# Attention and two expert layers on one core: a third query and key buffer, nine product buffers, weight conversion from slot 2

## The chip, the cores and the metric

The kernel runs on one core of a Trainium2 chip. The metric is device time in microseconds from start to end of one execution; the median of three timed runs of the kernel before is 641.99 us.

## The reference

Three layers run one after the other on 2304 tokens (4 batches of 576) of 512 values. The first is attention with 8 heads of 64: four heads look at the last 32 positions, four at every 32nd. The second multiplies by three matrices, takes the largest of the three products and multiplies by `w_out`. The third sends each token to the best of eight experts.

```python
def _attn_ref(q, k, v):
    ...
    scores = np.where(masks[None, :, :, :], scores, -1000000000.0)
    scores = scores - np.max(scores, axis=-1, keepdims=True)
    attn = np.exp(scores)
    attn = attn / (np.sum(attn, axis=-1, keepdims=True) + 1e-09)
    return np.matmul(attn, v)

def _moe_ref(x, w1, w2, w3, w_out):
    h = np.maximum(np.maximum(x @ w1, x @ w2), x @ w3)
    return h @ w_out

def _moe2_ref(x, modality_id, w_gate, modality_bias, w1, w2):
    logits = x @ w_gate + modality_bias[modality_id]
    e_idx = np.argmax(logits, axis=1)
    ...
        h = np.maximum(x[mask] @ w1[e], 0.0)
        out[mask] = gate_w[mask, None] * (h @ w2[e])
```

## The kernel before

Products are made from a high and a low half of each operand, three matmuls for one (`mm3`). Tokens are taken in six blocks of 384. For block j, `L1(j, f)` makes slice f (of six) of the first product of the second layer: three groups of twelve matmuls, m = 0, 1, 2, with the largest kept in `t1s`. `L2(j)` multiplies the six slices by `w_out` and gets six groups of eighteen. The slices of a block lie in `chunks`, buffers of 768 columns, taken in turn (`h_of`): eleven before.

Everything else is put between these matmul groups. `slot()` is one step of it; a list written out by hand in the last lines of the program decides how many slots there are, and the engines' queues take instructions in the order in which `slot()` writes them. Attention is cut into 40 groups. In a slot with a tick, slot t, group t gets its scores (`att_S`, TensorE), group t-1 its max and bias (VectorE), t-2 its exponential (ScalarE), t-3 its reciprocal (VectorE) and multiplication (GpSimd), t-4 its transposes, and t-5 its product with the values; the result of t-5 is written as a high half (`att_hi`, ScalarE) and a low half (`att_lo`, VectorE), and L1 reads both.

The weights of the second layer come as 24 pieces of 512 KB with 64-bit words and are converted to 32 bit. A slot with conversion takes piece i: the absolute value on ScalarE (`conv_abs`, line 366), four VectorE operations on piece i-1 (`conv_ops`, lines 378, 381, 383, 385; the last one frees the staging buffer, of which there are three, and the next piece is loaded), and the split of piece i-2 (line 397 on ScalarE, 398 on GpSimd). Pieces 18 to 23 are `w_out`; each also gets a transpose (`gate_T`, line 405) and four small matmuls (`gate_G`, line 411), which fold the experts' gate into `w_out`. These gate slots take accumulator banks from the same round as L1: two banks while conversion goes on, three afterwards (`mm_bank`).

The first thirteen slots are the prologue. No L1 runs there, since its first block needs groups 0 to 7; `keep_warm` puts four matmuls without use behind each slot. Before, conversion starts at slot 4 (`CS`). Loads are issued by the SyncE queue in the order of the slots: in slot t the next piece, the values of group t-2, and the queries and keys of group t+2 if that group is the first of a head pair. The two buffers `qk_b` hold a head pair each.

Of the kernel before, what the change touches and what calls it, by code (L numbers as in the profile page):

```python
# [10 lines left out]
F32 = mybir.dt.float32  # L11
F32R = mybir.dt.float32r
# [13 lines left out]
NF = DFF // 128  # L26
# [80 lines left out]
def tile_attention_moe_moe(ctx: ExitStack, tc: tile.TileContext, qk, vw, w, wg, ids, bias, e12, cst, out):  # L107
    nc = tc.nc
    PE, ACT, DVE, POOL, SP = nc.tensor, nc.scalar, nc.vector, nc.gpsimd, nc.sync
    sb = ctx.enter_context(tc.tile_pool(name="sb", bufs=1))  # L110
# [2 lines left out]
    W = sb.tile([128, 18432], F32R, name="W")  # L113
    R = sb.tile([128, 16384], F32R, name="R")
    HT = sb.tile([128, 4608], F32R, name="HT")
    HX = sb.tile([128, 3072], F32R, name="HX")
    stage = sb.tile([128, 3, 2, 512], F32, name="stage")
    y = sb.tile([128, NS, ROW], F32, name="y")
    t1s = sb.tile([128, 2, TB], F32, name="t1s")
# [32 lines left out]
    xh = R[:, xo:xo + KD * XR].rearrange("p (k t) -> p k t", k=KD)  # L152
    xl = R[:, xo + KD * XR:xo + 2 * KD * XR].rearrange("p (k t) -> p k t", k=KD)
    spare = R[:, xo + 2 * KD * XR:xo + 2 * KD * XR + 768]
    chunks = [z[:, 768 * i:768 * i + 768] for z, n in ((HT, 6), (HX, 4)) for i in range(n)] + [spare]

    def h_of(j, f):
        return chunks[(NF * j + f) % 11].rearrange("p (s t) -> p s t", s=2)

    ht = [HT[:, 768 * i:768 * i + 768].rearrange("p (s t) -> p s t", s=2) for i in range(6)]  # L160
    ht2 = ht + [W[:, 16384 + 768 * i:16384 + 768 * i + 768].rearrange("p (s t) -> p s t", s=2) for i in range(2)]
    at_pool = tc.tile_pool(name="at", bufs=1)
    AT = at_pool.__enter__().tile([128, 5504], F32, name="AT")
    qk_b = [AT[:, 1216 * i:1216 * i + 1216].rearrange("p (s n) -> p s n", s=2) for i in range(2)]
    v_b = [AT[:, 2432 + 384 * i:2432 + 384 * i + 384].rearrange("p (c d) -> p c d", c=3) for i in range(3)]
    s_b = [AT[:, 3584 + 384 * i:3584 + 384 * i + 384] for i in range(3)]
    pt_b = [AT[:, 4736 + 384 * i:4736 + 384 * i + 384].rearrange("p (c q) -> p c q", c=3) for i in range(2)]

    ew = [
        [z[:, o:o + 8192].rearrange("p (f m n) -> p f m n", f=NF2, m=2) for o in (0, 8192)]  # L170
# [15 lines left out]
    NG = len(groups)  # L186
    st = {}

    def load_qk(i):
        if i < NG and groups[i][2] == 0:  # L190
            b, p, _ = groups[i]
            SP.dma_start(qk_b[p % 2], qk[b, p])

    def load_v(i):
        if i < NG:
# [4 lines left out]
    def units(p, g):  # L200
        if p < 2:
            return [3 * g, 3 * g + 1, 3 * g + 2], 96
        return ([0, 3, 1, 4, 2, 5] if g == 0 else [6, 9, 7, 10, 8]), 54
# [3 lines left out]
    def mask_of(p, g, n):  # L207
        if p < 2:
            o = 0 if g == 0 else 96
            return mask[:, o:o + 288].rearrange("p (u k) -> p u k", k=96)  # L210
        return mask[:, None, 384:438].to_broadcast([128, n, 54])

    def s_view(i):
        b, p, g = groups[i]
        us, w_ = units(p, g)
        n = len(us)
        ps = bank[3 + i % 2][:, :n * w_].rearrange("p (u k) -> p u k", k=w_)
        wide = s_b[i % 3].rearrange("p (u k) -> p u k", k=96 if p < 2 else 64)
        m = mx[:, i % 4, :, :n]
        top = m[:, 0] if i in ON_DVE else bank[3 + i % 2][:, 400:400 + n]  # L220
        return ps, wide[:, :n, :w_], (top, m[:, 1], m[:, 2], m[:, 3]), n, w_
# [3 lines left out]
    def att_S(i):  # L225
        b, p, g = groups[i]
        us, _ = units(p, g)
        t = qk_b[p % 2]
        ps, _, _, n, w_ = s_view(i)
        pe = b < MASK_ON_PE  # L230
        if pe:
            PE.matmul(ps, lhsT=identb, rhs=mask_of(p, g, n))
        for c, u in enumerate(us):
            q0 = (64 if p < 2 else 54) * u
            for r in halves:
                PE.matmul(ps[r, c], lhsT=t[r, 0, q0:q0 + 64], rhs=t[r, 1, q0:q0 + w_], start=not pe, stop=True,  # L236
                          skip_group_check=pe)
# [108 lines left out]
    NW = NF * 3 + NF  # L346
# [4 lines left out]
    def load_piece():  # L351
        i = step["load"]
        if i < NW:
            step["load"] += 1
            SP.dma_start(stage[:, i % 3].rearrange("p a n -> p (a n)").bitcast(I32),
                         w[i].bitcast(I32))
# [8 lines left out]
    def conv_abs(i):  # L365
        ACT.activation(out=wbuf(i), in_=f32(conv_words(i)[1]), func=AF.Abs)
# [35 lines left out]
    def gate_T(a):  # L402
        ps = mm_bank()
        for kk in range(KD):
            PE.transpose(ps[:, 128 * kk:128 * kk + 128], a[:, 128 * kk:128 * kk + 128], ident)
        next_slot.append(lambda: ACT.copy(gate_t, ps))
# [11 lines left out]

    now = [0]
    DEPTH = 5  # L420
    CS, FILL = 4, 16
    later, delayed, next_slot = [], [], []

    def flush():
        while later:
            later.pop(0)()

    def slot(ticks=True, conv=True):

        flush()  # L430
        while next_slot:
            next_slot.pop(0)()
        t = now[0]
        i = step["conv"]
        ticks = ticks and t < NG + DEPTH
        conv = conv and i < NW + 3
        if ticks:
            now[0] += 1
        if conv:
            step["conv"] += 1  # L440
        at = lambda fn, d: fn(t - d) if ticks and 0 <= t - d < NG else None
        ops = conv_ops(i - 1) if conv else iter(())
        at(att_exp, 2)
        at(att_eps, 3)
        if conv and i < NW:
            conv_abs(i)
        next(ops, None)
        at(att_rec, 3)
        at(att_mul, 3)
        next(ops, None)  # L450
        at(att_max, 1)
        next(ops, None)
        at(att_bias, 1)
        for _ in ops:
            pass
        if conv and 0 <= i - 2 < NW:
            conv_split(i - 2)
        more = [delayed.pop() for _ in delayed[:]]

        def rest():  # L460
            if conv and NF * 3 <= i - 3 < NW:
                gate_G(i - 3 - NF * 3, bank[3 + t % 2][:, 384:384 + E])
            if conv and NF * 3 <= i - 2 < NW:
                gate_T(wbuf(i - 2))
            at(att_T, 4)
            at(att_V, 5)
            at(att_S, 0)
            at(att_pt, 4)
            at(att_hi, 5)
            at(att_lo, 5)  # L470
            for fn in more:
                fn()
            if ticks:
                if t >= 2:
                    load_v(t - 2)
                if t:
                    load_qk(t + 2)

        later.append(rest)

    mmi = [0]
# [363 lines left out]
    with tc.manual_schedule():  # L845
# [13 lines left out]
                PE.matmul(bank[0], lhsT=warm[:, :128], rhs=warm[:, :512])  # L859

        DVE.memset(t1s, 0.0)
        POOL.memset(AT[:, 3584:4736], 0.0)
        keep_warm(9)
        POOL.memset(filler, 1.0)
        for t in range(LEAD + DEPTH):
            slot(conv=t >= CS)
            flush()
            keep_warm(4)
            if t == 1:
                for v_ in range(2):  # L870
                    DVE.tensor_scalar(out=isf[:, v_], in0=idt[:, :, 0], scalar1=float(v_), scalar2=None, op0=ALU.is_equal)
                wide = lambda v_: isf[:, v_, :, None].to_broadcast([128, NT // 128, E])
                rep = lambda v_: bb[:, v_, None, :].to_broadcast([128, NT // 128, E])
                other = rt.rearrange("p a s e -> p (a s) e")
                POOL.tensor_tensor(out=ball, in0=wide(0), in1=rep(0), op=ALU.mult)
                POOL.tensor_tensor(out=other, in0=wide(1), in1=rep(1), op=ALU.mult)
                POOL.tensor_tensor(out=ball, in0=ball, in1=other, op=ALU.add)
            if t == 2:
                for _ in range(3):
                    load_piece()  # L880

# [4 lines left out]
        for j in range(NB):  # L888
            parts = [(L1, j, f) for f in range(NF)]
            if j:  # L890
                parts.insert(NF - 1 if j == 1 else 1, (L2, j - 1))
            n = sum(3 if p_[0] is L1 else 2 * NS for p_ in parts) - 2
            start = now[0]
            k = 0
            for fn, *arg in parts:
                for _ in fn(*arg):
                    k += 1
                    if FILL <= fills < FILL + E:
                        e_ = fills - FILL
                        SP.dma_start(xs[NT * e_:NT * e_ + TB].rearrange("(p s) (h n) -> p (s h) n", p=128, h=2),  # L900
                                     filler[:, None, :].to_broadcast([128, 2 * NS, ROW // 2]))
                    fills += 1
                    due = goal.get(j, start)
                    pieces = 10 + 12 * k // 16 if j == 0 else NW + 3
                    slot(now[0] < min(due, start - (start - due) * k // n), fn is L1 and step["conv"] < pieces)
                    background(6 if j == NB - 1 else 4)
                    if j == NB - 1 and arg[-1] >= 2 and fn is L1 and not behind and wts is None:
                        open_phase2()
                        load_rows(sp_val(e0i[0:1, 3:4], E * NT - TB))
                        wts = Weights(sp_val(e0i[0:1, 1:2], E - 1), 0)  # L910
# [58 lines left out]
```

## Time and profile before

| | us |
|---|---|
| median of three runs | 641.99 (641.83 to 642.63) |
| profiled execution | 642.13 |
| its span | 640.4 |
| TensorE busy (matmul) | 614.0 |
| VectorE busy | 257.6 |
| ScalarE busy | 229.9 |
| GpSimd busy | 136.0 |

The span runs from the first instruction to the last; the profiled execution's own time is 1.7 us longer. In the profile PE is TensorE (PEld its weight loads), DVE VectorE, ACT ScalarE, POOL GpSimd, and SPq the queue of SyncE, which issues loads. A start is in microseconds from the span's start; what stands in brackets is the engine's idle time before the instruction and what ended it.

### The profile page before, as it was taken

What the parts mean: (1) busy time and instruction counts of PE and PEld (TensorE: products, weight loads), DVE (VectorE), ACT (ScalarE), POOL (GpSimd) and SP (SyncE); (2) the same over time, 40 slices, a digit from 0 to 9 for tenths busy, and PEclk for the clock granted to TensorE, in tenths of its full rate; (3) what the DMA queues carried; (4) which work ended last, traced back from release to release, by engine and by line L of the source; (5) the groups of instructions that cost most, each with busy time, mean ns of one, the idle gap of its engine ahead of it and who ended that gap; (6) DMA issues with size and microseconds to landing.
All of it is one profiled execution on the core that took longest, in us unless ns stands there. A gap on an engine that the chain in (4) does not pass through costs nothing. (4 is left out here: it accounts for less than half of the span.)

```text
span 640.4 us, 11891 instructions
## 1 busy us (share of the span) xinstructions
PE 614.0 (96%) x4597; PEld 564.7 (88%) x4603; DVE 257.6 (40%) x701; ACT 229.9 (36%) x694; POOL 136.0 (21%) x157
## 2 busy tenths in 40 slices
PE   8889998999999999999999999999999999999992
PEld 4568988899999999999999999998998979898981
DVE  4987995331334333442131133374344215331210
ACT  2868755332244334333121111342343124422220
POOL 2445553221121321142112112101101010111000
PEclk9989999999999999999999999999999999999996
DMA  7686459982021312010000004244432127220201
GB/s 245 223 280 228 131 188 241 192 137 65 1 82 58 108 52 76 21 69 10 10 18 34 1 12 171 59 138 153 151 111 89 44 77 242 83 67 33 68 19 39
DMA packets 30668, 64.44 MB, mean 101 GB/s; under 512 B 3328, under 2 KB 14336, under 8 KB 30592
## 3 DMA queue, kind: packets, MB, share of 16 engines
q1 hardware_dynamic: 27712, 54.01, 29.6%
q0 software_dynamic: 2880, 9.46, 3.9%
q8 instruction: 43, 0.70, 0.5%
q14 instruction: 33, 0.27, 0.1%
HBM read 47.68 MB, written 15.77 MB: 99 GB/s over the span
## 5 line engine op out<-in xcount | busy, mean ns | idle before, releaser
L494 PE MATMUL bank<-R,W 128*128 128x384 f32 (+1 forms) x1350 | 253.3, 343 | 3.3 <-DVE t1s L513 2.0
L494 PEld LDWEIGHTS bank<-R,W 128*128 128x128 f32 x1350 | 235.8, 188 | 9.5 <-DVE t1s L513 3.0
L494 PE MATMUL bank<-R,HT 128*128 128x260 f32 (+1 forms) x540 | 89.9, 316 | 0.3 <-POOL HT L505 0.3
L513 DVE TENSOR_TENSOR t1s<-bank,t1s 128x384 f32<-128x384 f32 x72 | 40.1, 557 | 122.0 <-PE bank L494 120.8
L494 PEld LDWEIGHTS bank<-R,HT 128*128 128x128 f32 x540 | 78.0, 188 | 6.8 <-POOL HT L505 0.5
L717 POOL DMA_INDIRECT out_dram<-y,gi x18 | 18.0, 999 | 158.7 <-ACT x2h L698 94.9
L494 PE MATMUL bank<-x2h,R 128*128 128x384 f32 x192 | 49.5, 336 | 1.1 <-ACTq L925 1.1
L277 POOL TENSOR_TENSOR AT<-AT,mx 128x288 f32<-128x288 f32 (+2 forms) x40 | 27.1, 677 | 110.2 <-DVE mx L273 103.4
L494 PE MATMUL bank<-x2h,W 128*128 128x384 f32 x192 | 49.8, 337 | 0.0
L709 DVE SCALAR_TENSOR_TENSOR HT<-bank,HT 128x384 fp32r<-128x384 f32 x36 | 20.0, 557 | 64.0 <-ACT HT L708 63.7
L262 ACT ACTIVATE AT<-bank,mx 128x96 f32<-128x96 f32 (+1 forms) x138 | 42.9, 331 | 2.9 <-DVE R L415 1.7
L716 ACT ACTIVATE y<-bank,gi 128x512 f32<-128x512 f32 x18 | 12.4, 688 | 78.1 <-PE bank L494 64.7
L494 PE MATMUL bank<-W,HT 128*128 128x512 f32 x162 | 38.5, 391 | 0.0
L505 POOL TENSOR_TENSOR HT<-t1s,HT 128x384 fp32r<-128x384 f32 x21 | 21.3, 1014 | 72.9 <-ACT HT L504 72.8
L494 PEld LDWEIGHTS bank<-x2h,R 128*128 128x128 f32 x192 | 34.7, 188 | 1.6 <-ACTq L925 1.5
L494 PEld LDWEIGHTS bank<-W,HT 128*128 128x128 f32 x162 | 30.1, 188 | 6.0
L236 PE MATMUL bank<-AT 64*64 64x54 f32 (+1 forms) x640 | 31.2, 236 | 4.1 <-DMA AT<-in_qk_dram 3.4
L494 PEld LDWEIGHTS bank<-x2h,W 128*128 128x128 f32 x192 | 34.8, 188 | 0.3 <-issue 0.3
L708 ACT ACTIVATE HT<-bank 128x384 fp32r<-128x384 f32 x36 | 17.7, 492 | 47.0 <-PE bank L494 39.0
L236 PEld LDWEIGHTS bank<-AT 64*64 64x64 f32 x640 | 24.6, 134 | 10.4 <-DMA AT<-in_qk_dram 4.3
L343 DVE TENSOR_TENSOR R<-bank,R 128x162 fp32r<-128x162 f32 (+2 forms) x56 | 20.6, 397 | 32.2 <-ACT R L339 31.8
L511 ACT COPY t1s<-bank 128x384 f32<-128x384 f32 x36 | 17.3, 480 | 43.3 <-PE bank L494 38.6
(157 smaller groups left out, 807.1 us busy)
## 6 DMA issues: line engine op xcount, KB each, us to landing
stage<-in_w_dram SPq DMA_DIRECT2D x24, 512.0 KB, 4.1
stage<-in_e_dram SPq DMA_DIRECT2D x48, 256.0 KB, 3.7
AT<-in_qk_dram SPq DMA_DIRECT2D x15, 608.0 KB, 5.2
xs<-filler SPq DMA_DIRECT2D x8, 771.0 KB, 17.3
rows<-xs SPq DMA_DIRECT2D x7, 771.0 KB, 4.6
AT<-in_vw_dram SPq DMA_DIRECT2D x24, 144.0 KB, 3.4
AT<-in_vw_dram SPq DMA_DIRECT2D x16, 192.0 KB, 3.8
AT<-in_qk_dram SPq DMA_DIRECT2D x1, 352.0 KB, 4.6
```

Source lines behind the costliest of these rows:

```text
L236: PE.matmul(ps[r, c], lhsT=t[r, 0, q0:q0 + 64], rhs=t[r, 1, q0:q0 + w_], start=not pe, stop=True, skip_group_check=pe)
L262: ACT.activation(out=s3[:, c], in_=ps[:, c], func=AF.Exp, scale=0.125, bias=m[1][:, c:c + 1], accum_out=m[2][:, c:c + 1])
L277: POOL.tensor_tensor(out=s3, in0=s3, in1=m[3][:, :, None].to_broadcast([128, n, w_]), op=ALU.mult)
L343: DVE.tensor_tensor(out=l, in0=src, in1=f32(h), op=ALU.subtract)
L494: PE.matmul(ps, lhsT=a, rhs=b_, start=i == 0, stop=i == n - 1)
L505: POOL.tensor_tensor(out=h[:, 1], in0=t1, in1=f32(h[:, 0]), op=ALU.subtract)
L511: ACT.copy(t1, ps)
L513: DVE.tensor_tensor(out=t1, in0=ps, in1=t1, op=ALU.max)
L708: ACT.activation(out=h[:, 0], in_=ps, func=AF.Relu)
L709: DVE.scalar_tensor_tensor(out=h[:, 1], in0=ps, scalar=0.0, in1=f32(h[:, 0]), op0=ALU.max, op1=ALU.subtract)
L716: ACT.activation(out=y[:, s, :DM], in_=ps, func=AF.Copy, scale=gi[:, s, 0:1])
L717: POOL.indirect_dma_start(out=out[:, :], out_offset=bass.IndirectOffsetOnAxis(ap=gi[:, s, 1:2].bitcast(I32), axis=0), in_=y[:, s, :DM], in ...
```

## The change

There are three query and key buffers instead of two, taken in turn over all head pairs (`qk_of`), and a head pair is loaded three slots ahead instead of two. The space comes from the slices: nine buffers instead of eleven. With nine, L2 of block 0 stands behind the third slice of block 1, where it stood behind the fifth. Conversion starts at slot 2 (`CS`), the first three pieces are loaded one by one in slots 0 to 2 instead of together in slot 2, and the cap on converted pieces during block 0 is written anew: 11 pieces by the end of the prologue where there were 9, 21 by the end of block 0 where there were 23.

```diff
-    HX = sb.tile([128, 3072], F32R, name="HX")
+    HX = sb.tile([128, 1536], F32R, name="HX")
...
-    chunks = [z[:, 768 * i:768 * i + 768] for z, n in ((HT, 6), (HX, 4)) for i in range(n)] + [spare]
+    chunks = [z[:, 768 * i:768 * i + 768] for z, n in ((HT, 6), (HX, 2)) for i in range(n)] + [spare]
...
-        return chunks[(NF * j + f) % 11].rearrange("p (s t) -> p s t", s=2)
+        return chunks[(NF * j + f) % 9].rearrange("p (s t) -> p s t", s=2)
...
-    qk_b = [AT[:, 1216 * i:1216 * i + 1216].rearrange("p (s n) -> p s n", s=2) for i in range(2)]
+    qk_b = [AT[:, 1216 * i:1216 * i + 1216].rearrange("p (s n) -> p s n", s=2) for i in range(3)]
...
+    def qk_of(b, p):
+        return qk_b[(4 * b + (p + 2) % 4) % 3]
+
     def load_qk(i):
         if i < NG and groups[i][2] == 0:
             b, p, _ = groups[i]
-            SP.dma_start(qk_b[p % 2], qk[b, p])
+            SP.dma_start(qk_of(b, p), qk[b, p])
...
-    CS, FILL = 4, 16
+    CS, FILL = 2, 16
...
                 if t:
-                    load_qk(t + 2)
+                    load_qk(t + 3)
...
-            if t == 2:
-                for _ in range(3):
-                    load_piece()
+            if t < 3:
+                load_piece()
...
-                parts.insert(NF - 1 if j == 1 else 1, (L2, j - 1))
+                parts.insert(3 if j == 1 else 1, (L2, j - 1))
...
-                    pieces = 10 + 12 * k // 16 if j == 0 else NW + 3
+                    pieces = 11 + 10 * k // 17 if j == 0 else NW + 3
```

What this does to the queues shows at three places. The first is SyncE's queue at the start of the program; `in_qk` is queries and keys, `in_vw` values, `in_w` weight pieces, and the rows begin with the load for group 2. Before:

```order
L192 DMA AT<-in_qk_dram 128x1216
L851 DMA wgt<-in_wg_dram 128x32
L852 DMA bb<-in_bias_dram 128x16
L853 DMA y<-in_ids_dram 128x36
L198 DMA AT<-in_vw_dram 128x384
L192 DMA AT<-in_qk_dram 128x1216
L355 DMA stage<-in_w_dram 128x1024 x3
L198 DMA AT<-in_vw_dram 128x384 x2
L192 DMA AT<-in_qk_dram 128x1216
L355 DMA stage<-in_w_dram 128x1024
```

The same place after the change:

```order
L195 DMA AT<-in_qk_dram 128x1216
L854 DMA wgt<-in_wg_dram 128x32
L855 DMA bb<-in_bias_dram 128x16
L856 DMA y<-in_ids_dram 128x36
L358 DMA stage<-in_w_dram 128x1024
L195 DMA AT<-in_qk_dram 128x1216
L358 DMA stage<-in_w_dram 128x1024
L201 DMA AT<-in_vw_dram 128x384
L358 DMA stage<-in_w_dram 128x1024 x2
L201 DMA AT<-in_vw_dram 128x384
L195 DMA AT<-in_qk_dram 128x1216
```

The first weight piece now stands where the first load of values stood, and each further piece has a load of queries and keys or of values ahead of it.

The second place is VectorE's queue in slots 3 and 4 of the prologue: `mx` holds max, sum and reciprocal of a group, `y` the words of a piece, `bank_82` the piece half converted. Before:

```order
L268 TENSOR_REDUCE mx<-AT 128x6
L269 TENSOR_SCALAR mx<-mx 128x6
L273 RECIPROCAL mx<-mx 128x6
L244 TENSOR_REDUCE mx<-bank_83 128x6
L252 TENSOR_TENSOR bank_83<-bank_83,mx 128x324
L268 TENSOR_REDUCE mx<-AT 128x5
L269 TENSOR_SCALAR mx<-mx 128x5
L273 RECIPROCAL mx<-mx 128x5
```

After the change, from the same row on:

```order
L271 TENSOR_REDUCE mx<-AT 128x6
L272 TENSOR_SCALAR mx<-mx 128x6
L381 TENSOR_SCALAR y<-y 128x512
L276 RECIPROCAL mx<-mx 128x6
L384 TENSOR_SCALAR bank_82<-y 128x512
L247 TENSOR_REDUCE mx<-bank_83 128x6
L386 SCALAR_TENSOR_TENSOR bank_82<-stage,bank_82 128x512
L255 TENSOR_TENSOR bank_83<-bank_83,mx 128x324
L388 SCALAR_TENSOR_TENSOR y<-stage,bank_82 128x512
L271 TENSOR_REDUCE mx<-AT 128x5
```

The four conversion operations stand between the steps of the attention groups, the first of them ahead of the reciprocal and the max.

The third place is TensorE's queue where the last gate slots end, early in block 1; `bank_80` to `bank_82` are the accumulators of L1 and of the transposes. Before:

```order
L405 MATMUL bank_80<-cs,y 128x128 x4
L494 MATMUL bank_81<-R,W 128x384 x12
L411 MATMUL bank_83<-wgt,gate_t 128x8 x4
L405 MATMUL bank_80<-cs,w_96 128x128 x4
L494 MATMUL bank_81<-R,W 128x384 x6
L494 MATMUL bank_82<-R,W 128x384 x6
L411 MATMUL bank_83<-wgt,gate_t 128x8 x4
L494 MATMUL bank_82<-R,W 128x384 x6
```

After the change:

```order
L408 MATMUL bank_80<-cs,y 128x128 x4
L497 MATMUL bank_81<-R,W 128x384 x12
L414 MATMUL bank_83<-wgt,gate_t 128x8 x4
L408 MATMUL bank_80<-cs,w_96 128x128 x4
L497 MATMUL bank_81<-R,W 128x384 x12
L414 MATMUL bank_83<-wgt,gate_t 128x8 x4
```

A row of twelve is the second half of one L1 group and the first half of the next in the same bank. Behind the last transpose (the one from `w_96`) the group before changed to bank 82; after the change it stays in bank 81.

## Rows read from the trace of the kernel before

**Rows 1.** Windows: length; busy us of PE, PEld, DVE, ACT, POOL; clock; DMA; GB/s.

```profile
0.00:45.00 45.00, 37.27 (x460) 22.83 (x466) 34.10 (x98) 26.81 (x92) 18.33 (x26) 0.96 0.71 246
45.00:87.00 42.00, 41.87 (x408) 38.08 (x406) 36.90 (x86) 30.33 (x106) 21.53 (x21) 1.00 0.61 197
87.00:124.00 37.00, 32.75 (x256) 29.57 (x257) 21.70 (x48) 16.40 (x46) 13.54 (x13) 1.00 0.93 204
124.00:620.00 496.00, 493.72 (x3442) 467.66 (x3441) 164.88 (x472) 155.02 (x449) 80.61 (x96) 1.00 0.25 74
```

**Rows 2.** The timeline of PE at the prologue's end (start, us, operation, idle before).

```profile
36.13 1.16 PE L236 MATMUL bank<-AT 64*64 64x54 f32 x24 [2.32 <-DMA AT<-in_qk_dram]
37.22 1.89 PE L859 MATMUL bank<-t1s 128*128 128x512 bf16 x4
...
44.14 1.04 PE L859 MATMUL bank<-t1s 128*128 128x512 bf16 x4
44.82 3.52 PE L494 MATMUL bank<-R,W 128*128 128x384 f32 x18
```

**Rows 3.** The timeline of SP, the issuing of loads.

```profile
4.79 0.43 SPq L198 DMA_DIRECT2D AT<-in_vw_dram  x1
...
9.57 1.38 SPq L355 DMA_DIRECT2D stage<-in_w_dram  x3
...
26.58 0.38 SPq L198 DMA_DIRECT2D AT<-in_vw_dram  x1
...
30.48 0.42 SPq L192 DMA_DIRECT2D AT<-in_qk_dram  x1
```

**Rows 4.** The timeline of ACT, two weight pieces.

```profile
14.50 0.67 ACT L366 ACTIVATE y<-stage 128x512 f32<-128x512 f32 x1 [1.43 <-DMA stage<-in_w_dram]
...
37.77 0.67 ACT L366 ACTIVATE w<-stage 128x512 f32<-128x512 f32 x1 [1.22 <-DMA stage<-in_w_dram]
```

**Rows 5.** The timeline of DVE in the prologue.

```profile
11.50 0.50 DVE L244 TENSOR_REDUCE mx<-bank 128x6 f32<-128x324 f32 x1 [0.28 <-PE bank L236]
12.03 0.50 DVE L252 TENSOR_TENSOR bank<-bank,mx 128x324 f32<-128x324 f32 x1
...
15.20 0.43 DVE L378 TENSOR_SCALAR y<-y 128x512 f32<-128x512 f32 x1 [0.38 <-ACT y L366]
...
15.66 0.69 DVE L381 TENSOR_SCALAR bank<-y 128x512 int32<-128x512 int32 x1
16.27 0.46 DVE L244 TENSOR_REDUCE bank<-bank 128x3 f32<-128x288 f32 x1
...
18.63 0.78 DVE L343 TENSOR_TENSOR R<-bank,R 128x162 fp32r<-128x162 f32 x2 [0.59 <-ACT R L339]
...
40.79 0.36 DVE L343 TENSOR_TENSOR R<-bank,R 128x192 fp32r<-128x192 f32 x1 [1.64 <-ACT R L339]
...
44.16 0.36 DVE L343 TENSOR_TENSOR R<-bank,R 128x192 fp32r<-128x192 f32 x1 [0.23 <-ACT R L339]
```

**Rows 6.** The windows of two microseconds, columns as in the first group.

```profile
6.00:8.00 2.00, 1.74 (x29) 1.20 (x29) 0.57 (x2) 0.00 (x0) 0.00 (x0) 1.00 0.81 285
...
12.00:14.00 2.00, 1.84 (x26) 1.21 (x26) 1.86 (x6) 0.44 (x1) 0.65 (x2) 1.00 1.01 411
...
38.00:40.00 2.00, 2.00 (x12) 1.09 (x12) 1.15 (x3) 1.11 (x3) 0.98 (x1) 0.50 0.99 366
```

**Rows 7.** DMA issues near 4.8 us (KB, us to landing).

```profile
AT<-in_vw_dram SPq DMA_DIRECT2D x1, 192.0 KB, 4.5
```

**Rows 8.** The timeline of PE in the gate slots.

```profile
92.03 0.66 PE L405 MATMUL bank<-cs,y 128*128 128x128 f32 x4 [0.65 <-DVE t1s L513]
...
96.23 1.31 PE L494 MATMUL bank<-R,W 128*128 128x384 f32 x6 [0.62 <-ACT t1s L511]
```

**Rows 9.** The timeline of DVE, a conversion behind 45 us.

```profile
58.11 0.84 DVE L378 TENSOR_SCALAR w<-w 128x512 f32<-128x512 f32 x1
```

**Rows 10.** The timeline of POOL at the same time.

```profile
57.65 1.02 POOL L505 TENSOR_TENSOR HT<-t1s,HT 128x384 fp32r<-128x384 f32 x1
```

More of the change, by code (lines that the diff above doesn't have):

```diff
@@ L162, in tile_attention_moe_moe @@
     at_pool = tc.tile_pool(name="at", bufs=1)
-    AT = at_pool.__enter__().tile([128, 5504], F32, name="AT")
-    qk_b = [AT[:, 1216 * i:1216 * i + 1216].rearrange("p (s n) -> p s n", s=2) for i in range(2)]
-    v_b = [AT[:, 2432 + 384 * i:2432 + 384 * i + 384].rearrange("p (c d) -> p c d", c=3) for i in range(3)]
-    s_b = [AT[:, 3584 + 384 * i:3584 + 384 * i + 384] for i in range(3)]
-    pt_b = [AT[:, 4736 + 384 * i:4736 + 384 * i + 384].rearrange("p (c q) -> p c q", c=3) for i in range(2)]
+    AT = at_pool.__enter__().tile([128, 6720], F32, name="AT")
+    qk_b = [AT[:, 1216 * i:1216 * i + 1216].rearrange("p (s n) -> p s n", s=2) for i in range(3)]
+    v_b = [AT[:, 3648 + 384 * i:3648 + 384 * i + 384].rearrange("p (c d) -> p c d", c=3) for i in range(3)]
+    s_b = [AT[:, 4800 + 384 * i:4800 + 384 * i + 384] for i in range(3)]
+    pt_b = [AT[:, 5952 + 384 * i:5952 + 384 * i + 384].rearrange("p (c q) -> p c q", c=3) for i in range(2)]
     ew = [
@@ L227, in att_S @@
         us, _ = units(p, g)
-        t = qk_b[p % 2]
+        t = qk_of(b, p)
         ps, _, _, n, w_ = s_view(i)
@@ L861, in tile_attention_moe_moe @@
         DVE.memset(t1s, 0.0)
-        POOL.memset(AT[:, 3584:4736], 0.0)
+        POOL.memset(AT[:, 4800:5952], 0.0)
         keep_warm(9)
```

## Prediction

> **What bounds the kernel now.** Read the stretches first [rows 1]. TensorE is busy for 41.87 of the 42.00 us from 45 to 87 and for 493.72 of 496 us from 124 to 620: there it is the bound, and an earlier load or a lighter VectorE is worth nothing. Two stretches have room. From 87 to 124 TensorE is idle for 4.25 us. Up to 45 its work is mostly keep-warm matmuls: this prologue ends with the first L1 matmul at 44.82 [rows 2], and whatever moves that start moves the end one for one, since the work behind it is unchanged.
>
> What sets 44.82? [...] The transfer was issued at 30.48 [rows 3] and came 5.6 us later. VectorE's timeline tells the rest. From 18.63 to the end of the prologue it has two idle spells, 1.64 us before the low half of group 6 at 40.79 and 0.23 before that of group 7 at 44.16 [rows 5], and L1 needs that last one (44.16 and 0.36, then 44.82). So the prologue from about 19 us on is VectorE's queue, and the late transfer costs what VectorE lost by it: 1.64 + 0.23 = 1.87 us, not the 2.32 that TensorE waited.
>
> **The third query and key buffer** moves that transfer from the loads of slot 8 to those of slot 7. Slot 7's load of values was issued at 26.58 [rows 3]; right behind it, at about 27.0, with the longest trip seen (5.65 us) it lands at 32.7, before group 10 needs it (36.13 - 2.32 = 33.8). The wait goes. Gain: 1.9 us. Low bound 1.3: ScalarE was itself 1.22 us late at 37.77 for a weight piece [rows 4], and that would hold about half a microsecond of the low half of group 6. High bound 3.9, if TensorE and not VectorE sets the start: the 2.32 us wait and some 1.6 us of slow clock (0.85 on the keep-warm group alone, as much again on the groups about it).
>
> **Conversion from slot 2.** Two more pieces are converted before L1 starts. One costs VectorE an operation of 0.43 and three of 0.69 us, which start 0.61 apart where others stand between (15.66 to 16.27): 0.43 + 3 x 0.69 less the overlaps is 2.2 us, two are 4.3 [rows 5]. The same two sets leave the stretch after 45 us, where TensorE is the bound: no gain there. What covers them is VectorE's idle time in the early slots: 0.28, 0.38 and 0.59 us, 1.25 together [rows 5]. Interleaving hides a little more: alone, the subtract starts 0.53 behind its max (11.50 to 12.03); with a conversion operation between, the max takes its place in the queue and nothing waits for its result. I give that 0.5 for the two slots. Cost: 4.3 - 1.25 - 0.5 = 2.6 us.
>
> This holds if the first piece is there. In slot 2 it is issued where a 192 KB load of values stood, at 4.79, and that load landed 4.5 us later, at 9.3, behind everything else [rows 3, 7]. A piece has 320 KB more: at the 285 to 411 GB/s of the windows from 6 to 8 and from 12 to 14 [rows 6] that is 0.8 to 1.15 us, so it lands at 10.1 to 10.4; the absolute value on ScalarE takes 0.67 [rows 4], and VectorE starts at 11.1 at the latest, just where it was idle (11.2 to 11.5). Each microsecond later is one lost, since the absolute value stands in ScalarE's queue ahead of the exponential of group 1, and the conversion in VectorE's ahead of the max of group 2. Low bound of the cost 2.2 (landing at 10.1, one more hidden step). High bound 3.9: in the old burst a piece issued at 9.57 was used at 14.50, 4.9 us later with 608 KB ahead of it [rows 3, 4]. At 285 GB/s those 608 KB are 2.2 us, which leaves 2.7 where 512 KB should take 1.8: 0.9 us more, and 0.4 for the fourth piece, asked for only when the first is converted.
>
> [...] VectorE's first conversion operation takes 0.84 us at 58.11, against 0.43 at 15.20, while GpSimd works on another tensor from 57.65 to 58.67 [rows 5, 9, 10]. GpSimd gets two more splits in the prologue; if each meets such an operation the loss is 0.8, if none it is nothing. I take nothing, because the splits follow GpSimd's multiply and so mostly start after that operation, and leave the 0.8 to the range. [...]
>
> **Gate slots, 87 to 124.** In each of six slots a transpose of w_out takes one of two accumulator banks, and the next L1 group falls on the bank that its neighbour has just filled: 0.62 us at 96.23, the first of five such waits [rows 8]. The sixth is escaped because conversion has just ended and a third bank is free (bank 82 in the order of before). In the changed order the last of them reads bank 81 twelve times: a sixth wait, +0.65. Against it, the 0.65 at 92.03, a transpose waiting for VectorE [rows 8], falls in slots with one attention step less; I take 0.3 of it as gone. Together +0.3, between -0.5 and +0.9. **Nine product buffers and L2 of block 0 earlier** cost nothing: its w_out pieces are split and their gate columns done three slots before, and buffer f is written again only by L1(1,3), behind L2. The cover is the 2.3 us that TensorE idles in all of 124 to 620 [rows 1]; if it went wrong, one evacuation wait of 0.6.
>
> **Sum**, against the profiled execution's 642.13: -1.9 + 2.6 + 0.3 = +1.0, or 643.1; the median of the three runs stands 0.14 below it, so 643.0. Within 0.2% of 641.99, 640.7 to 643.3, is what a measurement can't tell from no change.
>
> **Rivals.** *The early weight pieces come late* (slower). DMA engines are already 0.81 busy from 6 to 8 us [rows 6], and the pieces now compete with the loads of queries and keys while ScalarE's queue stands behind them. For it: ScalarE waited for pieces at 14.50 and at 37.77. Against: the first piece only takes the place of a load that had landed by 9.3. With the cost at 3.9: 642.0 - 1.9 + 3.9 + 0.3 = 644.3. Chance 0.22.
>
> *TensorE sets the start* (faster). From 36.13 to 44.82 it has next to no idle time, so the whole 3.9 us might come back, and the conversions might fill VectorE's gaps best, at 2.2; with the gate slots unchanged 642.0 - 3.9 + 2.2 = 640.3. It decides from a cost below 2.6. Against it stand VectorE's rows: 0.3 us from the end of its last low half to L1, no gap from 18.63 to 40.79. Chance 0.15.
>
> *The transfer is late all the same*: the change doesn't do what it says. Shifted by 2.6 us, it is issued at 29.6 and needed at 36.4; a trip over 6.8 us, 1.2 more than the one in the rows, brings the wait back. 642.0 + 2.6 + 0.3 = 644.9. Chance 0.05.
>
> *My forecast*, 0.58, has a range of its own from 642.0 to 644.0; its upper part, 0.15 of it, is over the edge at 643.3. So faster 0.15, same 0.43, slower 0.15 + 0.22 + 0.05 = 0.42. The range takes in the middle of the faster case and nearly all of the slower ones: 640.6 to 645.0, with about 0.1 left out below and 0.05 above.
>
> **What will show it.** Group 10's scores wait for no transfer and the clock stays at full; ScalarE's first absolute value near 10.4 and VectorE's first conversion near 11.1; VectorE without a gap from there to the low half of group 7, near 44.9; L1's start at 45.2 to 45.8 instead of 44.82; six bank waits behind it. Wrong would be: L1 starting before 44.5 (then TensorE was the chain), ScalarE idle for two microseconds or more before its second or third piece (the slower rival), or an idle sum of TensorE in the stretch of the gate slots that differs from 4.25 by over a microsecond.

## The result, and the profile after

The changed kernel takes 650.07 us, median of four runs (649.28 to 657.15), beside 642.27 us for four runs of the kernel before: ratio 1.0132, 95% interval 1.0101 to 1.0164. The forecast was 643.0, with a range up to 645.0, so the direction that it held about as likely as no change came, and the size was missed by 7 us. The profiled execution took 649.87 us, its span is 648.1, and the difference of the two spans (640.4 before), 7.7 us, is what the trace has to explain.

The first group of rows answers to [rows 1]: length; busy us of PE, PEld, DVE, ACT, POOL; clock; DMA; GB/s. Windows of two microseconds from 120 on stand behind it.

```profile
0.00:45.00 45.00, 34.90 (x447) 20.94 (x455) 36.72 (x101) 27.23 (x92) 19.65 (x27) 1.00 0.76 261
45.00:87.00 42.00, 41.87 (x399) 37.64 (x395) 30.52 (x73) 27.38 (x100) 18.66 (x18) 1.00 0.52 172
87.00:124.00 37.00, 31.61 (x254) 28.49 (x251) 24.66 (x55) 16.86 (x47) 14.42 (x13) 0.96 0.92 212
124.00:620.00 496.00, 492.07 (x3433) 466.10 (x3433) 162.76 (x472) 154.92 (x451) 81.11 (x97) 1.00 0.25 74
...
118.00:120.00 2.00, 1.08 (x7) 0.76 (x5) 0.00 (x0) 0.65 (x2) 0.00 (x0) 1.00 1.03 349
120.00:122.00 2.00, 0.64 (x2) 0.64 (x3) 0.59 (x2) 2.00 (x7) 1.41 (x2) 0.76 1.10 291
122.00:124.00 2.00, 2.00 (x10) 2.00 (x8) 1.90 (x4) 0.38 (x1) 2.00 (x2) 0.50 1.26 163
124.00:126.00 2.00, 2.00 (x11) 2.00 (x11) 0.32 (x1) 0.17 (x1) 0.24 (x1) 0.50 1.14 153
126.00:128.00 2.00, 2.00 (x7) 1.51 (x6) 0.00 (x0) 1.10 (x2) 0.62 (x1) 0.53 1.04 163
```

The timeline of PE after the change (start, us, operation, idle before): the scores of group 10 and the first L1, which answer to [rows 2], and a stretch of the gate slots, which answers to [rows 8].

```profile
36.98 0.91 PE L239 MATMUL bank<-AT 64*64 64x54 f32 x24
37.82 1.04 PE L862 MATMUL bank<-t1s 128*128 128x512 bf16 x4
...
46.02 3.97 PE L497 MATMUL bank<-R,W 128*128 128x384 f32 x18
...
117.78 1.30 PE L497 MATMUL bank<-R,W 128*128 128x384 f32 x6
121.36 2.29 PE L497 MATMUL bank<-R,W 128*128 128x384 f32 x6 [2.28 <-ACT t1s L514]
123.45 1.71 PE L414 MATMUL bank<-wgt,gate_t 128*128 128x8 f32 x8
125.01 1.09 PE L408 MATMUL bank<-cs,y 128*128 128x128 f32 x4
125.76 2.25 PE L497 MATMUL bank<-R,W 128*128 128x384 f32 x6
128.66 1.32 PE L497 MATMUL bank<-R,W 128*128 128x384 f32 x6 [0.65 <-DVE t1s L516]
```

The prologue behaves nearly as forecast. Group 10's scores wait for nothing, the keep-warm group behind them takes 1.04 us, and the clock is 1.00 over the whole window to 45. L1 starts 1.20 us later than in [rows 2], and its first group takes 3.97 instead of 3.52 us. That is the smaller part, and one pair of traces does not fix it: four of the runs below have the prologue of the kernel before, and their L1 starts at 45.05, 46.68, 47.52 and 47.81. From the start of L1 to the end of the span there are 648.1 - 46.02 = 602.08 us, before 640.4 - 44.82 = 595.58: 6.5 us are lost behind the prologue, where the forecast had 0.3.

VectorE after the change, answering to [rows 5]: its first conversion, and its only idle spell from there to the end of the prologue.

```profile
11.64 0.43 DVE L381 TENSOR_SCALAR y<-y 128x512 f32<-128x512 f32 x1 [0.43 <-ACT y L369]
...
46.85 0.36 DVE L346 TENSOR_TENSOR R<-bank,R 128x192 fp32r<-128x192 f32 x1 [0.84 <-ACT R L342]
```

The lost time has its place in the rows of PE at 121.36. TensorE waits 2.28 us for an accumulator bank that ScalarE has not yet emptied. Right behind it the granted clock is 0.50 from 122 to 126: a half group takes 2.29 and 2.25 us where one takes 1.30 to 1.32 at a clock of 1.00.

Why was the bank not emptied? The timeline of ACT after the change, the prologue's first three pieces (which answer to [rows 4]), and the gate slot in question:

```profile
10.94 0.67 ACT L369 ACTIVATE y<-stage 128x512 f32<-128x512 f32 x1 [0.46 <-DMA stage<-in_w_dram]
...
13.65 0.66 ACT L369 ACTIVATE y<-stage 128x512 f32<-128x512 f32 x1 [1.76 <-DMA stage<-in_w_dram]
...
16.68 0.66 ACT L369 ACTIVATE y<-stage 128x512 f32<-128x512 f32 x1 [1.94 <-DMA stage<-in_w_dram]
...
119.35 0.66 ACT L369 ACTIVATE w<-stage 128x512 f32<-128x512 f32 x1 [4.97 <-DMA stage<-in_w_dram]
119.92 0.60 ACT L400 CAST R<-y 128x512 fp32r<-128x512 f32 x1
120.42 0.51 ACT L507 CAST HX<-t1s 128x384 fp32r<-128x384 f32 x1
120.84 0.47 ACT L514 COPY t1s<-bank 128x384 f32<-128x384 f32 x1
```

ScalarE stood 4.97 us in front of the absolute value of the last weight piece. The copy that empties the bank (L514) is the fourth instruction from there in its queue, and it ran 1.5 us after the piece had come. The copy's bank was full at 119.08 (117.78 + 1.30), and the copy ran at 120.84, behind the three instructions that stand ahead of it, the first of which waited for the piece until 119.35.

The piece is late because of where its load stands. The timeline of SP after the change; `xs<-filler` are the eight writes of 771 KB to DRAM that fill a table for the experts, one from each step from the 17th on (`FILL`):

```profile
97.25 0.33 SPq L358 DMA_DIRECT2D stage<-in_w_dram  x1
97.63 0.61 SPq L902 DMA_DIRECT2D xs<-filler  x1
101.49 0.34 SPq L358 DMA_DIRECT2D stage<-in_w_dram  x1
101.88 1.27 SPq L902 DMA_DIRECT2D xs<-filler  x2
105.53 0.34 SPq L358 DMA_DIRECT2D stage<-in_w_dram  x1
```

The DMA issues of the changed kernel at 105.5 (KB, us to landing):

```profile
stage<-in_w_dram SPq DMA_DIRECT2D x1, 512.0 KB, 13.7
```

And SP at the same place of the kernel before, which [rows 3] did not reach:

```profile
98.04 0.33 SPq L355 DMA_DIRECT2D stage<-in_w_dram  x1
98.47 3.04 SPq L900 DMA_DIRECT2D xs<-filler  x3
```

Before, the last piece goes out just ahead of the fillers and lands in 5.0 us. After, the new cap lets the last two pieces go out only behind the first and behind the third filler; the last one stands behind three writes of 771 KB, of which the first was nearly done (it landed at 106.1), and takes 13.7 us.

### The profile page after: what moved, and what is told of

Its sections match the earlier page's. It is cut to its first block, busy times and chain, and to the rows that moved or that the text cites. A ratio compares the mean times of both kernels' runs of the same rounds, so it can differ in the third digit from the quotient of the medians.

```text
span 648.1 us, 11896 instructions
## 1 busy us (share of the span) xinstructions
PE 616.4 (95%) x4597; PEld 566.2 (87%) x4603; DVE 256.5 (40%) x701; ACT 229.9 (35%) x694; POOL 136.8 (21%) x157
## 5 line engine op out<-in xcount | busy, mean ns | idle before, releaser
L497 PE MATMUL bank<-R,W 128*128 128x384 f32 (+1 forms) x1350 | 256.1, 345 | 6.1 <-DVE t1s L516 3.3
L497 PEld LDWEIGHTS bank<-R,W 128*128 128x128 f32 x1350 | 237.1, 189 | 13.7 <-DVE t1s L516 5.0
L497 PE MATMUL bank<-R,HT 128*128 128x260 f32 (+1 forms) x594 | 95.4, 313 | 0.0
L497 PEld LDWEIGHTS bank<-R,HT 128*128 128x128 f32 x594 | 84.0, 188 | 6.3
L508 POOL TENSOR_TENSOR HT<-t1s,HT 128x384 fp32r<-128x384 f32 x24 | 24.9, 1039 | 43.0 <-ACT HT L507 42.9
L497 PE MATMUL bank<-x2l,W 128*128 128x384 f32 x96 | 32.3, 336 | 0.0
L497 PE MATMUL bank<-x2l,R 128*128 128x384 f32 x96 | 32.2, 336 | 0.0
```

The lines of the kernel that those rows point to most:

```text
L497: PE.matmul(ps, lhsT=a, rhs=b_, start=i == 0, stop=i == n - 1)
L508: POOL.tensor_tensor(out=h[:, 1], in0=t1, in1=f32(h[:, 0]), op=ALU.subtract)
```

## The experiments

They ran on two chips in three groups; each is compared with the kernel before, run with its group on the same chip (643.37, 642.37 and 643.43 us, medians of 28, 21 and 18 runs). Theory A is what the rows above suggest: cap, late piece, bank, clock. The rivals are in the expectations. "From L1 to the end" is the profiled span less the start of the first L1, so it speaks of one run, while times and ratios are medians of several.

**Late piece or cap?** The first run moves the fillers, the second gives the cap back; both otherwise the changed kernel.

```diff
-    CS, FILL = 2, 16
+    CS, FILL = 2, 19
```

> The changed kernel, but the eight filler writes start three matmul groups later, behind the load of the last weight piece. Theory A, the last piece waited behind three filler writes (13.7 us from issue to landing) and so ScalarE, the bank and TensorE: the 2.28 us wait shrinks to the 0.65 of its neighbours and the slow clock of 121 to 128 us, about 3.2 us, goes; 4.8 us less than the changed kernel, 644.0 to 646.5. Theory B, the six conversions in a row and the sixth bank wait make the loss: within 1 us of the changed kernel, 649 to 651. Theory C, nine product buffers and the earlier L2: the same 649 to 651.

645.77 us, ratio 1.0051 (1.0033 to 1.0070). From L1 to the end 643.1 - 45.87 = 597.23, which is 4.85 less than in the changed kernel; the timed ratios, 1.0132 and 1.0051, lie 5.2 us apart. The last piece now goes out ahead of the fillers; it and the two before it land in 3.6 us (median of the three). The same half group in this run's timeline of PE:

```profile
119.55 1.32 PE L497 MATMUL bank<-R,W 128*128 128x384 f32 x6 [0.57 <-ACT t1s L514]
```

2.28 - 0.57 = 1.71 us of waiting are gone, and the slow rows at 121.36, 123.45, 125.01 and 125.76 give back 0.97 + 0.76 + 0.46 + 0.95 = 3.14 against their durations at full clock (1.32, 0.95, 0.63, 1.30): 4.85 in all.

```diff
-                    pieces = 11 + 10 * k // 17 if j == 0 else NW + 3
+                    pieces = 10 + 12 * k // 16 if j == 0 else NW + 3
```

> The changed kernel with the cap on converted pieces that the kernel before had, so that the last pieces are loaded and converted in the same matmul groups as before. Theories A and B: all of the loss behind the prologue goes and its 1.2 us stay, 643.0 to 644.5. Theory C, nine product buffers and the earlier L2: 648 to 651.

643.86 us, ratio 1.0014 (1.0002 to 1.0027); from L1 to the end 642.6 - 47.66 = 594.94. With the old cap the rest of the change costs 0.9 us, and nine buffers with the earlier L2 lose nothing behind the prologue.

**The late piece without the cap.** The kernel before, fillers begun three steps earlier.

```diff
-    CS, FILL = 4, 16
+    CS, FILL = 4, 13
```

> The kernel before, but the filler writes start three matmul groups earlier, so that three of them stand ahead of the last weight piece as in the changed kernel. Theory A: the same wait and slow clock appear, 645.5 to 648.5, with a ScalarE wait of 3 us or more for the last piece. Theories B and C: no more than 643.5.

644.53 us, ratio 1.0008 (0.9991 to 1.0025). Theory A missed in size: this time is not clear of noise, and the run that was profiled, 646.42 us, is the slowest of the ten. So what this run shows is the order in its trace. The last piece again stands behind three fillers: issued at 101.19, it is used at 114.80, 13.6 us later, where ScalarE waits for it. The timeline of ACT and, last, of PE:

```profile
106.89 0.67 ACT L366 ACTIVATE y<-stage 128x512 f32<-128x512 f32 x1 [4.24 <-DMA stage<-in_w_dram]
...
114.80 0.67 ACT L366 ACTIVATE w<-stage 128x512 f32<-128x512 f32 x1 [3.17 <-DMA stage<-in_w_dram]
...
117.47 1.33 PE L494 MATMUL bank<-R,W 128*128 128x384 f32 x6 [1.44 <-DVE t1s L513]
```

ScalarE waits for two pieces, but TensorE only 1.44 us instead of 0.65, and the clock stays at 1.00. From L1 to the end it is 596.79, 1.2 more than before. Behind the second of these pieces stands no copy of an L1 bank but the high half of an attention group (`att_hi`); VectorE waits for that, and TensorE for VectorE. So here the late piece cost by what stood behind it in ScalarE's queue.

**The parts alone.** First the third buffer, with the loads three slots ahead, nine product buffers and the earlier L2, but `CS`, the loads of the first pieces and the cap as before:

```diff
-    CS, FILL = 2, 16
+    CS, FILL = 4, 16
...
-            if t < 3:
-                load_piece()
+            if t == 2:
+                for _ in range(3):
+                    load_piece()
...
-                    pieces = 11 + 10 * k // 17 if j == 0 else NW + 3
+                    pieces = 10 + 12 * k // 16 if j == 0 else NW + 3
```

> The changed kernel with conversion from slot 4, the three pieces loaded together and the cap as before: what is left is the third query and key buffer, the load one slot earlier, nine product buffers and the earlier L2. As forecast, VectorE's queue sets the start of L1, so 1.9 us are gained: 640.0 to 641.2, L1 from 42.6 to 43.4. Rival, TensorE sets it: 638.0 to 639.0, L1 near 41. Rival, the wait is only moved: 642.0 to 642.6.

640.27 us, ratio 0.9963 (0.9942 to 0.9984): faster than both kernels. L1 starts at 42.95; from there to the end 637.9 - 42.95 = 594.95.

Then, in the kernel before, the cap alone (the cap's line as in the change) and the early conversion alone (`CS` 2 and the loads one by one, as in the change):

> The kernel before with the new cap alone (11 + 10k/17); everything else as before. Theory A (the cap moves the loads of the last weight pieces behind the first filler writes; ScalarE waits for the last one, the copy that frees an accumulator bank stands behind it, TensorE waits over two microseconds and its clock falls): the loss appears in full without any other part of the change. From the first L1 to the end of the span 601 to 602.5 us where before it was 595.6, so 6 us over the kernel before, a ratio near 1.0095. Rival B (the new cap costs bank waits and denser late slots alone, as in the run with later fillers): 597 to 598 us from the first L1, ratio 1.0025 to 1.004. Rival C (the cap matters only together with the nine buffers and the earlier L2): no difference from before, 595 to 596 us.

649.51 us, median of four (646.70 to 654.60), ratio 1.0132 (1.0079 to 1.0185): within this interval the cap alone costs as much as the whole change. But the profiled run was the fastest of the four, and does not show all of it: ScalarE waits 3.91 us for the piece, TensorE 1.22, the clock behind it stays at 1.00, and from L1 to the end there are 644.9 - 46.68 = 598.22 us, near what rival B expects. The timeline of ACT, then of PE:

```profile
119.28 0.66 ACT L366 ACTIVATE w<-stage 128x512 f32<-128x512 f32 x1 [3.91 <-DMA stage<-in_w_dram]
...
121.28 1.32 PE L494 MATMUL bank<-R,W 128*128 128x384 f32 x6 [1.22 <-ACT t1s L511]
```

The other three runs took 649.15 to 654.60, so this was tried again below.

> The kernel before with conversion from slot 2 and the three pieces loaded one by one alone: two query and key buffers, eleven product buffers, old cap. By the prediction's cost term (two more pieces of 2.2 us on VectorE, 1.75 hidden): first L1 2.6 us later than in the kernel before, at 47.4, ratio near 1.004; if the late transfer for group 10 is hidden behind the longer VectorE queue, the cost is 2.6 less 1.9, the start 45.5, ratio near 1.001. Rival (the early pieces come late and ScalarE's queue stands): start 48.0 or later and waits of ScalarE for the first three pieces over 4 us together. All of this holds for a first query and key load that lands as in the kernel before; where TensorE waits about 2 us for it and its clock falls around 8 to 10 us, the start is 1.5 to 3 us later whatever the kernel. From the first L1 to the end 595 to 596.

646.89 us, ratio 1.0064 (1.0036 to 1.0091). The timeline of PE:

```profile
7.80 0.56 PE L236 MATMUL bank<-AT 64*64 64x54 f32 x12 [1.29 <-DMA AT<-in_qk_dram]
...
40.28 1.53 PE L236 MATMUL bank<-AT 64*64 64x54 f32 x24 [2.16 <-DMA AT<-in_qk_dram]
...
48.84 3.52 PE L494 MATMUL bank<-R,W 128*128 128x384 f32 x18
```

L1 starts 4.02 us later than before. 1.01 of that is the first query and key load, which here releases its scores at 7.80 and in the kernel before at 6.79; the other 3.0 are what the conversions cost by this pair of traces, where two buffers make group 10 wait as well (2.16 us). The figure is loose: from that release to L1 it is 48.84 - 7.80 = 41.04 us here and 38.03 in the kernel before, but 38.09, 39.25, 39.69 and 39.94 in four more runs with the prologue of the kernel before. The timed runs lie 4.1 us apart, with an interval of 2.3 to 5.8. ScalarE's waits for the first three pieces are 3.4 us together. From L1 to the end 595.66, as before.

**A later start, for a version that wins.** The third buffer alone with `CS` 5, and with 6:

> The kernel with the third buffer alone (conversion from slot 4, old cap, first pieces loaded together), conversion started at slot 5 instead. One piece fewer on VectorE ahead of L1: by the price of 2.2 us a piece the first L1 comes up to 2 us earlier than the 42.95 of slot 4, at 41 to 42, if VectorE still sets the start. The piece goes to block 0, where TensorE was busy for 41.87 of 42 us; if VectorE has room there (it was busy for 36.9 of 42 us), from the first L1 to the end stays at 595 and the time falls by 1 to 2 us (ratio to the kernel before about 0.993). Rival: VectorE's queue in block 0 fills and TensorE waits for it, or the last piece falls behind the fillers: 596 us or more from the first L1, no gain.

> The same with conversion started at slot 6: two pieces fewer on VectorE ahead of L1. If VectorE sets the start, first L1 at 39 to 40.5; more likely the loads of values and the attention steps on ScalarE and TensorE take over as the bound and it comes at 41. Its two pieces, 4.3 us of VectorE, go to block 0, which leaves VectorE about 41 of 42 us busy there: 596 to 598 us from the first L1, time 0 to 1 us below that of slot 5. Rival: a matmul group of block 0 waits for its weights and the clock falls: 600 us or more from the first L1.

641.28 us, ratio 0.9983 (0.9960 to 1.0006), and 642.60 us, 1.0004 (0.9986 to 1.0023). L1 starts at 41.57 and 40.96, but 596.63 and 599.74 us follow. The windows of slot 5, then of slot 6:

```profile
45.00:87.00 42.00, 41.22 (x401) 36.78 (x400) 37.32 (x87) 32.10 (x113) 23.28 (x22) 1.00 0.61 197
```

```profile
45.00:87.00 42.00, 38.91 (x377) 33.98 (x374) 38.55 (x86) 30.52 (x104) 22.61 (x21) 1.00 0.59 198
```

TensorE, busy for 41.87 us of this stretch in [rows 1], loses 0.65 and 2.96 us in it. The rival holds: what leaves the prologue has to be paid in block 0. Of the starts tried (2, 4, 5, 6) slot 4 has the lowest times; its interval overlaps that of slot 5, so those two are not told apart.

**Three runs more.** The cap alone again, to see the slow stretch; the cap with the fillers later (`FILL` 19, in the kernel before); the third buffer alone on another chip.

> The kernel before with the new cap alone, a second look: its timed runs stood at the time of the whole change, but the run that was profiled was its fastest and showed the wait behind the late piece at 1.22 us and no slow clock. Theory A: where the run takes 648 us or more, the trace shows ScalarE waiting 4 us or more for a piece near 117 us, TensorE waiting two microseconds or more behind it, and a granted clock near 0.5 for some 6 us right after; from the first L1 to the end 601 to 603. Rival (the lost time of the slower runs sits elsewhere, as in a slow prologue): the stretch from 115 to 130 us stays at full clock and the first L1 starts after 48 us.

651.66 us for two runs, ratio 1.0134 (1.0071 to 1.0197); the profiled one took 656.11. Its timeline of ACT, then of PE:

```profile
120.65 0.66 ACT L366 ACTIVATE w<-stage 128x512 f32<-128x512 f32 x1 [4.46 <-DMA stage<-in_w_dram]
...
122.14 0.48 ACT L511 COPY t1s<-bank 128x384 f32<-128x384 f32 x1
...
122.67 1.32 PE L494 MATMUL bank<-R,W 128*128 128x384 f32 x6 [1.78 <-ACT t1s L511]
...
125.87 2.27 PE L494 MATMUL bank<-R,W 128*128 128x384 f32 x6
```

And its windows:

```profile
122.00:124.00 2.00, 1.33 (x9) 1.34 (x9) 1.25 (x3) 1.69 (x5) 2.00 (x2) 1.00 1.15 193
124.00:126.00 2.00, 2.00 (x12) 2.00 (x12) 1.56 (x3) 0.17 (x1) 1.55 (x2) 0.53 1.18 162
...
142.00:144.00 2.00, 2.00 (x22) 1.90 (x20) 0.21 (x1) 0.24 (x1) 0.99 (x1) 0.50 0.67 166
144.00:150.00 6.00, 6.00 (x34) 6.00 (x33) 1.28 (x3) 0.75 (x3) 0.00 (x0) 0.95 0.22 84
```

The chain of theory A is there in full without any other part of the change. The wait is shorter than expected (1.78 against two or more) and the slow clock far longer: half speed from 124 to 144, not for six microseconds. From L1 to the end 654.3 - 47.52 = 606.78, above the expected 601 to 603.

> The kernel before with the new cap and the fillers begun three slices later (behind the last weight piece). Theory A: the late piece and the slow clock are gone, what is left of the cap is a sixth bank wait and waits of the denser gate slots: 596.5 to 597.5 us from the first L1 to the end, ratio to the kernel before 1.001 to 1.003. Rival (the cap itself, by conversions in other slots, makes the loss): ratio 1.010 or more, as with the cap alone.

647.19 us, ratio 1.0047 (1.0026 to 1.0069). With the fillers later, 5.6 us of the cap's loss are gone from the timed runs (ratio 1.0134 and 1.0047): the late piece was the larger part. In the profiled run the clock stays full in the gate slots, and from L1 to the end it is 642.6 - 45.05 = 597.55, so the denser slots cost 597.55 - 595.58 = 2.0 us there. The ratio is above the expected 1.003: the profiled run, 644.37, is among the fastest of the nine, and where the five runs of 647 to 648 us lost more was not traced.

> The kernel with the third buffer, the loads three steps ahead, the nine product buffers and the earlier L2, but conversion from slot 4 and the old cap, a second time on another chip beside the kernel before: if its gain is real, first L1 near 43 us, 595 us from there to the end, a ratio of 0.994 to 0.998. Rival (the gain of the first time was a matter of when the first query and key load landed): ratio within 0.002 of one.

640.21 us, ratio 0.9956 (0.9939 to 0.9972). The gain is real; this profiled run starts L1 at 41.36 and has 595.04 us behind it.

## Why the prediction was wrong

**The step that failed is the one on the gate slots**, "Together +0.3, between -0.5 and +0.9". It counted bank waits and priced none of the loads. The new cap was read for its number of pieces at each end, and the change's own order on SyncE's queue was followed at the program's start alone, so that the last piece passed behind three fillers unpriced. What this cost, from the rows: in the changed kernel TensorE's idle times between 88 and 137 sum to 7.29 us, in the kernel before to 4.12, which is +3.17; the slow clock adds 3.14. Together 6.3 us, beside the 6.5 that were lost from L1 on; the longer first group is 0.45 more, and 0.26 was gained elsewhere. Of these 4.85 are the late piece (shown by the run with later fillers), the rest the denser slots. With the cap given back the timed ratio falls from 1.0132 to 1.0014.

**The bank waits themselves.** The sixth came, as predicted. With the late piece away TensorE idles 5.60 us in this stretch against 4.12: +1.5, of which 0.56 are bank waits and 0.92 others, two of about 0.6 before the gate's small matmuls (for ScalarE's work on the attention group) and one of 0.61 for GpSimd's split of a piece. The 0.65 at 92.03 is gone, but more came than went. So even without the late piece the term would have been 1.5 and not 0.3.

**The third buffer, -1.9 (1.3 to 3.9).** Right in mechanism and near in size: alone it gains 2.4 and 2.8 us by the timed runs (ratios 0.9963 and 0.9956), of which, by the traces, some 0.6 are gained behind the prologue. Counted from the scores that the first late query and key load releases (7.53 and 6.53 with the buffer alone), L1 comes after 35.42 and 34.83 us, and in the five traces with two buffers and conversion from slot 4 after 38.03 to 39.94: 2.6 us or more. Whether TensorE's own wait and its slow clock, which the forecast left to the high bound, came back in part can't be told from so wide a spread.

**Conversion from slot 2, +2.6 (2.2 to 3.9).** Too small, though within its range: the runs with the old cap and with the third buffer alone differ in this term only, on one chip, and their medians by 643.86 - 640.27 = 3.6 us. By the count above it is 46.02 - 7.00 = 39.02 in the changed kernel against 34.83 to 35.42, so 3.6 to 4.2, and 45.87 - 7.64 = 38.23 in the run with later fillers, so 2.8 to 3.4. The first absolute value (10.94 for 10.4) and VectorE's first conversion (11.64 for 11.1) are half a microsecond late, and VectorE works without a gap until 46.85, where it idles 0.84 behind a ScalarE that waited 0.83 for a piece. The rival of late early pieces saw its waits (1.76 and 1.94 us, just under the two that were its sign); how much of the price is theirs was not tried apart. In sum the two terms of the prologue were +0.7, and with the old cap the whole kernel is 0.9 us slower. The sum held, in part by luck: conversion cost 1.0 us more than forecast, and the third buffer with the nine product buffers gained 0.5 to 0.9 more.

**VectorE beside GpSimd, 0.** In the changed kernel none of the ten VectorE operations of this kind up to 45 us takes longer than 0.43 us. Behind 45 us the 0.84 that the prediction took from the kernel before is one of six there, of 0.59 to 1.01 us; in that trace GpSimd was at work when each of the six began, but what lengthens them was not shown. **Nine buffers and the earlier L2, 0.** No loss: 594.94 to 595.04 us from L1 on in three runs. They are even 0.6 below the kernel before; what gives this was not tried apart.

**The range** was too narrow at the failed step: no rival let the gate slots lose more than 0.9, and the clock's fall was priced in the prologue only, though [rows 2, 6] showed it behind a wait of 2.32 us, just such a wait as came here.

## What to carry to other kernels

When a cap or a schedule moves a load, follow the issuing queue to the last load that moves, and look for bulk writes that it now stands behind; then name what is queued behind its consumer. In this kernel three writes ahead of one piece made 4.85 of the 6.5 us that were lost behind the prologue. And take a change apart before dropping it: the third buffer without the rest is 0.4% faster than the kernel that it was to improve.

## What the runs showed of the hardware

A 512-KB load took 4.1 to 5.0 us just ahead of the first filler, 6.2 us behind one of them, and 13.7 us behind three on the same SyncE queue, while the busy share of the DMA engines stood at 1.12 to 1.21 and they moved 125 to 177 GB/s from 110 to 116, against 411 GB/s in the prologue from 12 to 14 [rows 6]. Whether the load is late because it waits in its queue for the writes ahead of it, or because the writes keep the DMA engines busy, was not shown: no run put the load on another queue.

The clock is the larger surprise. In the gate slots, one trace each, a wait of TensorE of 2.28 us was followed by half clock for about seven microseconds (0.50 to 0.53 from 122 to 128), one of 1.78 by twenty (0.50 to 0.53 from 124 to 144), one of 1.22 or 1.44 by none (1.00 from 120 to 128 and from 116 to 124). One and the same kernel differed by several microseconds from run to run: the cap alone took 646.7 us at a mean clock of 0.988 and 656.1 at 0.973. That the slowest run of the changed kernel, 657.15, had such a long stretch is likely from its mean clock (0.974; in the traced run of the cap alone that took 656.11 it is 0.973), but it was not traced. At the program's start the same happens: where the second half of the first scores waited 1.78 to 2.02 us for its load, the clock stood at 0.50 to 0.60 from 8 to 10 us and L1 came at 47.5 to 47.8 (three runs).
